# Four instead of six plain feature groups in a two-layer spectral and dense kernel, with regrouped quads and reordered row transfers

## The chip, the cores and the metric

The kernel runs on one core of one Trainium2 chip. The metric is the device time of one execution in microseconds, lower is better. The span of a profile runs from the first to the last instruction on the core; the execution's time is a little longer.

## What is computed

Two layers, each a spectral part and a dense part, on a residual stream x of 2048 tokens by 1024 features in bf16:

```python
x = x + _A_ref(_layernorm(x, axis=-1), A_w_r, A_w_i)
x = x + _B_ref(_layernorm(x, axis=-1), B_w1, B_b1, B_w2)
x = x + _A_ref(_layernorm(x, axis=-1), A_w_r, A_w_i)
x = x + _B_ref(_layernorm(x, axis=-1), B_w1, B_b1, B_w2)

def _A_ref(x, w_r, w_i):
    X = rfft2(x.astype(float32), axes=(-2, -1))
    return irfft2(X * (w_r + 1j * w_i), s=(S, D), axes=(-2, -1)).astype(bfloat16)

def _B_ref(x, w1, b1, w2):
    h = einsum("bsd,df->bsf", x, w1) + b1
    sp = log1p(exp(-abs(h))) + where(h > 0, h, 0)
    return einsum("bsf,fd->bsd", h * tanh(sp), w2)
```

The dense part has 3584 hidden features. Its activation is one table function (Mish) on ACT.

## The kernel before

The order of the work is written out by hand. A `Prog` object per engine collects instructions in program order; every tile has a `Res` that remembers who wrote and read it, and from these the waits follow. So each engine (and SP, which issues most DMAs, and POOL, which issues some and also computes) is one in-order queue, and an instruction's place in the program is its place in the queue.

**Spectral part** (`layer_A`). Stages of small matrix products. The first, `s1` (L635 on PE, evictions L641 on ACT and L643 on DVE), reads the tile XR, which holds all tokens in another order; the last, the inverse transform `i4` (L1020), reads the tile UT, 32 KB per partition from offset 64 K. `i4` for tokens 0 to 511 comes first; the rest (`rest`, fifteen or ten columns at a time) is woven into the beginning of the dense part, and its results go through the staging tile YS into the residual stream (`residual`, L1396).

**Dense part** (`layer_B`). Tokens are in four chunks of 512. Pass 0 covers chunks 0 and 1, pass 1 chunks 2 and 3. In each pass the first product makes 14 feature groups of 256 features. There are two ways to make a group:

- *plain*: `mm1` (L1148), 16 matmuls of 512 columns for each chunk, so 32 a group; a chunk can be halved into 256 columns. Three PSUM banks rotate, and ACT's Mish (L1152) empties them.
- *quad*: `quads` (L1186), a scheme of Strassen's kind with seven products of four matmuls, 28 a group. The products are named by their operands: A11*B11, A12*B21, A22*T4, S2*T2, S4*B22, S1*T1, S3*T3. A are quarters of the group's weights, S1 to S4 are sums of such quarters, B are parts of the two chunks, T1 to T4 are differences of such parts. A11*B11 and A12*B21 read chunk 0 alone. DVE makes T1 to T4 (`token_sums`, L1163). T3 is written over part of chunk 1. Each quad has one p1 copy on ACT (L574), five adds on DVE (L1191) and four Mishes on ACT (L1196).

The weight sums S1 to S4 of a group are made once, by POOL (L1081, four operations), in a slot of 7168 bytes that holds weights and sums, and stored to scratch; later passes load the slot from scratch. `fill_slot` does all of this. In layer 0, pass 0 makes the groups that it takes as quads, and pass 1 makes the others. POOL's first sums of pass 0 wait for a gate: DVE's last normalization of chunk 1. Slots WE0 to WE3 lie where UT lay, WS0 to WS2 where the plain groups' weights lie.

In pass 0 before the change, groups 0 to 5 are plain and 6 to 13 are quads. Chunk 1 is being normalized and transposed while chunk 0 is multiplied. Normalization of a tile of 128 tokens needs statistics (on DVE with bn_stats, L472, or on ACT with two summing passes, `stats_act`, L453), scales (8 small DVE operations, L502 to L515; after ACT statistics three more, L464 to L466), and `apply` (L524). Then the tile is transposed by PE (`transposed`, L1109, evicted by DVE, L1114) or by eight DMAs on SP (`turned` and `turn`).

Then `products` makes the second product (L1268) in seven stages of four tiles; a helper `extra` runs between its tiles.

**The boundary between the layers.** At the end of layer 0, each tile is normalized and stored as rows to scratch (`xn_store`, POOL), and loaded from there into XR (`xr_load`, SP). The last tile, 15, goes to XR directly in sixteen small DMAs (`xr_direct`, half k by block h). `xr_load(14)` waits for the store of tile 14. Meanwhile `spin` runs matmuls that nobody reads on PE.

```python
1601:                b = self.apply(j, out=True)
1602:                if j < 15:
1603:                    self.xn_store(j, b)
1604:                if j > 8:
1605:                    self.xr_load(j - 1)
1606:                if j == 15:
1607:                    self.xr_direct(j, b, 2, (pool, act, sp))
```

## Time and profile before

| what | us |
|---|---|
| median of 9 runs | 938.07 (936.67 to 940.18) |
| profiled execution | 936.9 |
| its span | 935.1 |
| mean granted TensorE clock | 0.989 |

| stage of layer 0 (us from the span's start) | from | to |
|---|---|---|
| plain groups of pass 0, chunk 0 and 1 | 123.7 | 173.5 |
| quads of pass 0 | 173.5 | 220.3 |
| second product of pass 0 | 220.3 | 307.6 |
| quads of pass 1 | 307.6 | 392.3 |
| second product of pass 1 | 397.1 | 478.5 |
| idle PE after the spin, layer boundary | 483.8 | 489.3 |

The costliest groups of instructions, as the page lists them (line, engine, operation, output from inputs, count; then busy time and mean duration in ns; then the engine's idle time ahead of them and what ended most of it):

```profile
L1268 PE MATMUL PS<-ARENA 128*128 128x512 bf16 x1536 | 338.0, 379 | 1.7
L1186 PE MATMUL PS<-ARENA 128*128 128x512 f16 (+1 forms) x1210 | 266.6, 379 | 2.1 <-POOL ARENA L1081 1.0
L1191 DVE TENSOR_TENSOR ARENA<-PS,ARENA 128x512 f32<-128x512 f32 x220 | 151.7, 691 | 96.2 <-PE PS L1186 92.1
L1196 ACT ACTIVATE ARENA<-ARENA,B 128x512 bf16<-128x512 f32 x132 | 95.0, 721 | 67.2 <-DVE ARENA L1191 61.1
L1148 PE MATMUL PS<-ARENA 128*128 128x256 bf16 (+1 forms) x570 | 86.7, 308 | 0.5
L1081 POOL TENSOR_TENSOR ARENA<-ARENA 128x512 bf16<-128x512 bf16 x56 | 71.3, 1274 | 73.8 <-DVE ARENA L524 59.0
```

Matmuls overlap, so their mean of 379 ns is a latency; the distance between two of them is shorter. Idle time of an engine that others don't wait for costs nothing.

### The profile page before, as it was taken

The page shows a single profiled execution, that of the slowest core. Times are in us where ns is not written, and L with a number is a line of the kernel's source. Part 1 is how long each engine was busy: PE and PEld are TensorE (multiplying, and loading weights), DVE is VectorE, ACT ScalarE, POOL GpSimd, SP SyncE. Part 2 cuts the span into 40 slices and gives each one's busy share as a digit, 9 for nine tenths or more (in the row PEclk, how much of TensorE's full clock was granted, in tenths as well). Part 3 has the DMA queues.
Part 4 walks back from the last instruction along what each step waited for, and adds up shares of the span by engine and source line. Part 5 has one row for each costly group of instructions (what it writes and reads, how often), then busy time and mean ns, then how long its engine had stood idle before and what let it go on. Part 6 is the DMA issues. An engine that isn't in the chain of part 4 may idle for free.

```text
span 935.1 us, 13406 instructions
## 1 busy us (share of the span) xinstructions
PE 871.5 (93%) x5398; PEld 471.7 (50%) x5473; DVE 618.9 (66%) x973; ACT 427.4 (46%) x623; POOL 158.4 (17%) x183
## 2 busy tenths in 40 slices
PE   0799789999999999999978987999999999999998
PEld 0676476444444444444437765754444444444443
DVE  7697468686889667568746865647746665554473
ACT  7798486456203475420008975745551015552000
POOL 3922003960004641010130200000000000000000
PEclk9999999999999999999989998999999999999999
DMA  9969854675796388364640798333155635832442
GB/s 289 265 222 295 206 139 126 215 273 144 259 277 230 139 309 292 116 242 142 252 149 32 223 228 198 158 118 119 54 187 170 213 113 191 279 120 77 169 127 112
DMA packets 146335, 174.68 MB, mean 187 GB/s; under 512 B 66248, under 2 KB 125736, under 8 KB 146152
## 3 DMA queue, kind: packets, MB, share of 16 engines
q1 hardware_dynamic: 133424, 127.48, 44.6%
q0 software_dynamic: 10672, 44.67, 13.3%
q10 hardware_dynamic: 2176, 1.66, 0.6%
q8 instruction: 43, 0.70, 0.3%
q14 instruction: 20, 0.16, 0.1%
HBM read 130.00 MB, written 40.89 MB: 183 GB/s over the span
## 4 chain that ended last, share of the span: by engine, by line
PE 81%; DMA 6%; DVE 5%; POOL 3%; ACT 2%; issue 1%; SPq 1%; POOLq 0%; DVEq 0%; ACTq 0%
PE PS L1268 34%; PE PS L1186 26%; PE PS L1148 9%; POOL ARENA L1081 2%; PE PS L799 2%; PE PS L725 2%; PE PS L1020 2%; PE PS L824 2%; DMA ARENA<-in_B_w_dram 1%; PE PS L1109 1%; DMA XS<-in_A_x_dram 1%; DMA ARENA<-c_bt 1%; POOL ARENA L251 1%; DMA ARENA<-u_scratch 1%; ACT ARENA L641 1%
## 5 line engine op out<-in xcount | busy, mean ns | idle before, releaser
L1268 PE MATMUL PS<-ARENA 128*128 128x512 bf16 x1536 | 338.0, 379 | 1.7
L1186 PE MATMUL PS<-ARENA 128*128 128x512 f16 (+1 forms) x1210 | 266.6, 379 | 2.1 <-POOL ARENA L1081 1.0
L1268 PEld LDWEIGHTS PS<-ARENA 128*128 128x128 bf16 x1568 | 153.3, 98 | 184.6 <-DVE ARENA L1311 0.3
L1191 DVE TENSOR_TENSOR ARENA<-PS,ARENA 128x512 f32<-128x512 f32 x220 | 151.7, 691 | 96.2 <-PE PS L1186 92.1
L1186 PEld LDWEIGHTS PS<-ARENA 128*128 128x128 bf16 x1232 | 120.2, 98 | 147.2 <-POOL ARENA L1081 2.6
L1196 ACT ACTIVATE ARENA<-ARENA,B 128x512 bf16<-128x512 f32 x132 | 95.0, 721 | 67.2 <-DVE ARENA L1191 61.1
L574 ACT ACTIVATE ARENA<-PS 128x512 f32<-128x512 f32 (+2 forms) x82 | 61.1, 745 | 119.2 <-PE PS L1186 96.4
L1148 PE MATMUL PS<-ARENA 128*128 128x256 bf16 (+1 forms) x570 | 86.7, 308 | 0.5
L1081 POOL TENSOR_TENSOR ARENA<-ARENA 128x512 bf16<-128x512 bf16 x56 | 71.3, 1274 | 73.8 <-DVE ARENA L524 59.0
L453 ACT ACTIVATE ARENA<-XS 128x1024 bf16<-128x1024 bf16 x52 | 54.8, 1053 | 37.0 <-DVE XS L1319 33.0
L1148 PEld LDWEIGHTS PS<-ARENA 128*128 128x128 bf16 x576 | 55.5, 98 | 26.7 <-DVE ARENA L1114 0.9
L1293 DVE TENSOR_TENSOR ARENA<-ARENA 128x3584 bf16<-128x3584 bf16 x32 | 63.9, 2016 | 0.0
L1319 DVE TENSOR_TENSOR XS<-PS,ARENA 128x512 bf16<-128x512 f32 x52 | 35.7, 689 | 38.5 <-PE PS L1268 38.2
L1152 ACT ACTIVATE ARENA<-PS,B 128x256 bf16<-128x256 f32 (+1 forms) x72 | 38.4, 542 | 35.6 <-PE PS L1148 35.0
L1311 DVE TENSOR_TENSOR ARENA<-PS,ARENA 128x512 f32<-128x512 f32 x48 | 32.9, 687 | 28.4 <-PE PS L1268 28.0
L1196 ACT ACTIVATE ARENA<-PS,B 128x512 bf16<-128x512 f32 x44 | 30.2, 686 | 18.0 <-PE PS L1186 18.0
L1307 DVE TENSOR_TENSOR ARENA<-ARENA,XS 128x512 f32<-128x512 f32 x52 | 36.7, 730 | 0.5
L1163 DVE TENSOR_TENSOR ARENA<-ARENA 128x2048 f16<-128x2048 bf16 x16 | 25.3, 1581 | 17.6 <-PE PS L1148 17.3
L799 PE MATMUL PS<-ARENA 128*128 128x256 bf16 x256 | 32.4, 273 | 4.2 <-DVE ARENA L788 3.2
L472 DVE BATCH_NORM_STATS2 BN<-XS 128x6 f32<-128x512 bf16 x52 | 32.7, 671 | 4.7 <-DMA XS<-in_A_x_dram 4.7
L444 ACT ACTIVATE RS<-MV,EPS 128x1 f32<-128x1 f32 (+2 forms) x11 | 3.3, 296 | 70.7 <-DVE MV L565 70.0
L777 ACT ACTIVATE ARENA<-PS 128x1024 bf16<-128x1024 f32 x32 | 33.3, 1071 | 4.5 <-PE PS L773 4.5
(97 smaller groups left out, 815.0 us busy)
## 6 DMA issues: line engine op xcount, KB each, us to landing
ARENA<-in_B_w_dram SPq DMA_DIRECT2D x30, 896.0 KB, 6.4
ARENA<-w1s_scratch SPq DMA_DIRECT2D x30, 896.0 KB, 4.8
ARENA<-w2s_scratch SPq DMA_DIRECT2D x24, 896.0 KB, 6.6
ARENA<-in_B_w_dram SPq DMA_DIRECT2D x26, 512.0 KB, 5.3
w1s_scratch<-ARENA POOLq DMA_DIRECT2D x14, 896.0 KB, 4.3
u_scratch<-ARENA SPq DMA_DIRECT2D x14, 512.0 KB, 3.5
ARENA<-u_scratch SPq DMA_DIRECT2D x14, 512.0 KB, 5.7
w2s_scratch<-ARENA POOLq DMA_DIRECT2D x8, 896.0 KB, 4.2
```

The costliest lines, as they stand in the source:

```text
L453: self.op(act, lambda e, i=i, f=f: e.activation(junk.ap, x, f, accum_out=sums[:, i:i + 1]), reads=[self.r_xs[j]], writes=[junk.res], parts ...
L574: fn = (lambda e: e.activation(dst, src, ACT.Copy)) if scale is None else \
L799: fns.append(lambda e, c=c, part=part: e.matmul(ps[:, c * 256:(c + 1) * 256], yk.ap[:, part, c * P:(c + 1) * P], t[:, (128, 0)[part]:(384, ...
L1081: self.op(self.pool, lambda e, dst=A(dst), x=A(x), y=A(y), op=op: e.tensor_tensor(dst, x, y, op), reads=[b.res] + list(after), writes=[b.rs])
L1148: fns.append(lambda e, db=db, bank=bank, fl=fl: e.matmul(PS[:, bank, 0:w], wb.ap[:, db, fl * P:(fl + 1) * P], x.ap[:, db, tok], start=(db ...
L1152: self.op(act, lambda e, bank=bank, ft=ft, at=at: e.activation(at[:, tok], PS[:, bank, 0:w], ACT.Mish, bias=self.B1[:, ft:ft + 1]), reads= ...
L1186: self.group([lambda e, db=db: e.matmul(PS[:, bank, :], A[:, db, :], mov[:, db, :], start=(start and db == 0), stop=(db == 3), skip_group_ ...
L1191: self.op(dve, lambda e: e.tensor_tensor(dst.ap, PS[:, bank, :], x.ap, ALU.add), reads=[self.r_bank[bank], x.res], writes=[dst.res])
L1196: self.op(act, lambda e: e.activation(at, src, ACT.Mish, bias=self.B1[:, ft:ft + 1]), reads=[res, self.r_b1], writes=[ra])
L1268: self.group([lambda e, i=i, k=k, b=PB[n][k].ap: e.matmul(PS[:, bank, :], ap[:, i, t * P:(t + 1) * P], b[:, i - 7 * k, :], start=(start an ...
L1293: self.op(dve, lambda e: e.tensor_tensor(ap[dst][:, f, :], ap[x][:, f, :], ap[y][:, f, :], op), reads=part(x, k) + part(y, k), writes=part ...
L1307: self.op(dve, lambda e: e.tensor_tensor(a[t], a[t], x, ALU.add), reads=[rx], writes=[r[t]])
```

## The change

Pass 0 of both layers: groups 0 to 3 are plain, 4 to 13 are quads.

- The places of plain groups 4 and 5 on chunk 0 are taken by the one-chunk products of quads 0 to 3: A11*B11 of all four (`block`) and A12*B21 of quads 1 to 3 (`corner`), in banks 3, 4, 5 and 0; the corner of quad 0 stays in its quad. Two more p1 buffers hold their copies.
- Slots WE0 to WE3 get their raw weights right after the last `rest` (`fill_raw`), and their sums behind the gate as before (`fill_sums`). For that UT's resource is split into four quarters by address.
- Products that read no sum no longer wait for the sums, in all passes.
- Tiles 6 and 7 have their residual ahead of 4 and 5, and their ACT statistics one group earlier. The transposes of tiles 6 and 7 stand in the third plain group of chunk 1 instead of the second.
- Tiles 8 to 11 have their statistics on ACT instead of DVE and their scales in two pairs; in layer 0 the residuals of tiles 10 and 11 move into the quads.
- In layer 1 tiles 13 and 14 are transposed by DMA instead of PE; before, in both layers, 13 to 15 are PE's.
- At the boundary `xr_direct(15)` is issued ahead of `xr_load(14)`, with another order of queues, and the spin has 38 matmuls instead of 24.

The core of the diff:

```diff
 def xr_direct(self, j, b, parts, queues):
+        b.unread = False
...
-            self.r_ut = self.sub_res(self.UT, "ut", 4, o["UT"], P * P * 2)
+            self.r_ut = [self.sub_res(self.UT, f"ut{q}", 1, o["UT"] + P * 64 * q, P * 64)[0] for q in range(4)]
...
-        self.w1_buf = [... for i in range(6)]
-        for fg in range(6):
+        self.w1_buf = [self.alloc(f"W1_{i}", self.ob["WS"] + i * 4096, [8, 256]) for i in range(4)]
+        for fg in range(4):
...
+    def fill_raw(self, b, fg):
+        r = self.r_w1d[fg]
+        if r.writes:
+            self.dma(self.sp, b.ap[:, 0:2048], self.w1s_d[fg][:, 0:2048], f"w1_{b.res.name}", reads=[r], writes=[b.res])
+        else:
+            self.load_w1(b.raw, fg, [b.res])
+    def fill_sums(self, b, fg, after):
+        r = self.r_w1d[fg]
+        if r.writes:
+            self.dma(self.sp, b.ap[:, 2048:3584], self.w1s_d[fg][:, 2048:3584], f"w1s_{b.res.name}", reads=[r], writes=[b.rs])
+        else:
+            self.w1_sums(b, fg, after)
...
+            p1_of = sums[0:2] + [self.alloc(f"P1_{off}", off, [512], F32) for off in spare]
+            ready = range(len(p1_of)) if spare else ()
...
-                            for db in range(4)], reads=[s.res, s.rs] + list(res), writes=[self.r_bank[bank]])
+                            for db in range(4)], reads=[s.res] + [s.rs] * (a[0] == "S") + list(res), writes=[self.r_bank[bank]])
...
+            def block(n, bank=None):
+                a, b, d, p1, u2, u3, ft = parts(n)
+                a = a if bank is None else bank
+                product(n, a, "A11", "B11", True)
+                self.copy(act, p1.ap, PS[:, a, :], [self.r_bank[a]], [p1.res])
+            def corner(n, bank=None):
+                a, b, d, p1, u2, u3, ft = parts(n)
+                a = a if bank is None else bank
+                product(n, a, "A12", "B21", False)
+                mish(0, ft, PS[:, a, :], self.r_bank[a])
...
+                        if n not in ready:
+                            block(n)
                         product(n, b, "S2", "T2", True)
...
                         product(n, d, "S1", "T1", True)
+                        if n not in ready:
+                            corner(n)
+                        elif n == 0:
+                            corner(0, 3)
                         product(n, b, "S3", "T3", False)
...
-        for j in range(4, 8):
+        early = self.open_slots("WE", self.ob["W2"], 0, 1, 2, 3)
+        for n in range(4):
+            self.fill_raw(early[n], 4 + n)
+        for j in (6, 7, 4, 5):
             residual(j)
...
             mm1(0, fg, 1)
-            if fg > 1:
-                self.stats_act(4 + fg)
-        mm1(0, 4)
+            if fg < 3:
+                self.stats_act(5 + fg)
         at_tiles(1)
-        mm1(0, 5, mid=turns(1, 0, 1))
+        block, corner, run = quads(list(range(4, 14)), order, B, [k * 1024 for k in (102, 140)])
+        for n, bank in ((0, 3), (1, 4), (2, 5), (3, 0)):
+            block(n, bank)
+        corner(1, 4)
+        for f in turns(1, 0, 1):
+            f()
+        corner(2, 5)
+        corner(3, 0)
...
-            self.fill_slot(early[n], 6 + n, [gate])
-        for fg in range(2):
-            mm1(1, fg, 0, mid=turns(1, 2, 3) if fg else ())
-        for fg in range(2):
+            self.fill_sums(early[n], 4 + n, [gate])
+        for fg in range(3):
+            mm1(1, fg, 0, mid=turns(1, 2, 3) if fg == 2 else ())
+        for fg in range(3):
             mm1(1, fg, 1)
...
         def after(n):
-            if n == 0:
-                self.fill_slot(order[7], 13)
+            if n in (0, 4, 5):
+                k = (7, 8, 9)[(0, 4, 5).index(n)]
+                self.fill_slot(order[k], 4 + k)
...
-            if n < 4:
-                self.stats_dve(8 + n)
-            if n == 4:
-                self.scales(8, 4)
-            if n > 3:
-                normal(4 + n)
+            if n in (0, 2, 4, 5):
+                self.stats_act(8 + (0, 2, 4, 5).index(n))
...
+            if n in (5, 7):
+                self.sums_to_mv(n + 3, 2)
+                self.scales(n + 3, 2)
+            if n > 5:
+                normal(2 + n)
                 turn(4)
-            for j in ((), (), (), (), (), (12, 13), (14,), (15,))[n]:
+            for j in {2: () if last else (10,), 4: () if last else (11,), 7: (12, 13), 8: (14,), 9: (15,)}.get(n, ()):
                 residual(j)
...
+        by_pe = 15 if last else 13
...
-                normal(12)
-                for j in (13, 14, 15):
+                for j in range(12, by_pe):
+                    normal(j)
+                for j in range(by_pe, 16):
                     xn[j] = self.apply(j)
...
+                else:
+                    self.xr_direct(j, b, 2, (act, pool, sp, act, pool, act, pool, sp) * 2)
                 if j > 8:
                     self.xr_load(j - 1)
-                if j == 15:
-                    self.xr_direct(j, b, 2, (pool, act, sp))
...
-            self.spin(24, 7)
+            self.spin(38, 7)
```

## The prediction

> **What bounds the kernel now.** I read the busy shares, then PE's waits, then the timeline of each engine around pass 0 of the dense stage in layer 0 (114 to 222 us; the same stage of layer 1 lies 455 us later), then the chain of waits at the layer boundary (478 to 500 us).
>
> The page's busy line, then who made PE wait:
>
> ```profile
> PE 871.5 (93%) x5398; PEld 471.7 (50%) x5473; DVE 618.9 (66%) x973; ACT 427.4 (46%) x623; POOL 158.4 (17%) x183
> ...
> PE PS L635 <- DMA ARENA<-ARENA: 5.4, 1, 5.4
> ...
> PE PS L1186 <- POOL ARENA L1081: 1.0, 3, 0.4
> ```
>
> The timelines of ACT, POOL and DVE (start, us, instruction):
>
> ```profile
> 142.59 1.05 ACT L453 ACTIVATE ARENA<-XS 128x1024 bf16<-128x1024 bf16 x1
> ...
> 144.82 0.82 ACT L1152 ACTIVATE ARENA<-PS,B 128x256 bf16<-128x256 f32 x2
> ...
> 154.06 6.57 POOL L1081 TENSOR_TENSOR ARENA<-ARENA 128x512 bf16<-128x512 bf16 x4 [58.99 <-DVE ARENA L524]
> ...
> 173.77 2.50 DVE L1163 TENSOR_TENSOR ARENA<-ARENA 128x2048 f16<-128x2048 bf16 x1 [5.82 <-PE PS L1148]
> ...
> 628.77 1.23 DVE L1163 TENSOR_TENSOR ARENA<-ARENA 128x2048 f16<-128x2048 bf16 x1 [11.46 <-PE PS L1148]
> ...
> 667.75 1.28 DVE L1396 TENSOR_TENSOR XS<-XS,ARENA 128x1024 bf16<-128x1024 bf16 x2
> 669.28 1.42 DVE L1191 TENSOR_TENSOR ARENA<-PS,ARENA 128x512 f32<-128x512 f32 x2 [0.24 <-PE PS L1186]
> ```
>
> The chain of waits at the boundary, and one row of PE's busy time by windows (behind the counts: clock, DMA share, GB/s):
>
> ```profile
> 481.97 0.60 SPq L251
> ...
> 483.20 5.85 DMA ARENA<-ARENA
> ...
> 486.50:488.00 1.50, 0.00 (x0) 0.00 (x0) 0.00 (x0) 0.00 (x0) 0.00 (x0) 0.50 0.82 164
> ```
>
> The reader is to see: PE is the bound (93%), so a matmul saved is time saved unless another engine makes PE wait. In the dense stages it waits for almost nothing, 1.0 us in all for POOL's sums. Each tile's ACT statistics hold ACT 2.23 us (142.59 to 144.82). POOL makes the four sums of a group in 4.87 us (a later row), and in 6.57 while DVE works on bf16 too; DVE's last token sum takes 2.50 us beside POOL and 1.23 alone. After a quad's third add, DVE has about 2 us before the next pair of adds. At the boundary PE is idle 5.45 us and restarts at half clock (0.50).
>
> **What the skill says.** The Trainium skill, *TensorE: Matmul & The Clock Gate*, Part 1, gives 215.7 ns for a warm matmul of 512 columns: here DVE's pairs of adds recur every 6.04 us in the quads (651.15 to 657.19), which is 28 matmuls at 0.216. It also says that the gate judges activity in free-running windows of 3413 ns; the clock here stays at half until about 493.0, one full window after work resumes. *SBUF — State Buffer*, "SBUF: two separate sides", says that VectorE and GpSimd share a port pair as an exclusive lock; 2.50 against 1.23 us agrees. *DMA: Bandwidth & Descriptors*, "Queues, rings and completion order", says that each engine consumes a queue's descriptors in ring order; in the trace SP's small row packets mostly come after the 32 KB packets of the load issued ahead of them.
>
> **The change, part by part.** I call four matmuls of 512 columns a product: 0.863 us.
>
> *Plain work saved, each layer.* Two groups of pass 0 go from plain (32 matmuls) to quads (28): 8 x 0.2158 = -1.73 us.
>
> *ACT statistics a group earlier.* Tile 6's now follow group 1's Mishes on ACT, tile 7's group 2's. ACT is free at 140.94; tile 6 occupies it to 143.17, and group 2's first Mish ends near 143.6. The fourth group's second half reuses that Mish's bank (mm1 rotates three) and would start at 142.87. Queued behind the statistics: both Mishes of group 2, hence PE. Wait +0.8 per layer (0.4 to 0.9). The p1 copies that follow (0.5 each) finish just as the corner product needs them. The transposes of tiles 4 and 5 then stand at 148.9, as before, after DVE's apply (148.15).
>
> *Early raw loads.* Slots 0 and 1 load while the inverse transform still runs; 2 and 3 wait for its last product (138.5). Two 0.5 MB loads, by a row of 5.3 us landing, are there near 144.5; blocks 2 and 3 need them at 145.4 and later. Cost 0, up to 1 without that cover. Splitting UT's resource is what lets 0 and 1 go; the split fill, the ring flag and the closures issue no other work.
>
> *T3 in layer 0.* T3 overwrites chunk 1's data, so it waits for the last plain product. Four products (3.45 us) cover T3 and the add behind it today; the block is gone, three remain (2.59). T3 2.42 to the next start, 0.29 delay, add 0.68: 3.4. Wait +0.4 to +0.85; I take +0.6, since POOL's gap for a store issue (0.56) falls there. Layer 1: 1.23 in place of 2.42, covered.
>
> *Short quads.* Quads 1 to 3 have five products (4.32 us). A22 of the quad before waits for an add that ends 0.92 after S3, and only S2 (0.86) lies between: 3 x 0.09 = +0.27 per layer (0 to 0.5). ACT and DVE otherwise fit: five adds are 3.45.
>
> *POOL in layer 0.* Its gate stays at 153.97, the sums still take 5.75 us a group with the store issue, but the quads start at 166.5 instead of 173.5 and the short ones need a slot each 4.4 us. POOL: slots done near 160.6, 167.5, 173.4, 179.2, 185.1; PE wants them at 166.5, 170.6, 175.0, 179.4, 184.7. Wait about +0.6 at quads 3 and 4, with the later ones just in time (0 to 6, see the rival). Block and corner products no longer wait for sums.
>
> *Scales by pairs.* After quad 7, DVE gets 11 small operations (0.198 each, 2.18), an apply (0.46) and two residuals (1.28) in one gap: 3.92 us from phase 4.05 of a 6.04 us period, so the next adds start 1.87 late. Block and S2 give them 0.75 to 0.8 of slack. +1.08 per layer (0.8 to 1.9; more if POOL still sums then, but its last sums end near 214.2, and the residuals start near 215.5). After quad 5 the lateness is 0.2 to 0.7, inside the slack. DVE loses four tiles' bn_stats and ACT gains 9 us, inside its idle 54%, with copies up to 1.2 us later, which the next adds absorb.
>
> *Pass 1 of layer 0.* Groups 4 and 5 now come from scratch instead of POOL, and A11 no longer waits for its sums: PE's three waits (0.35, 0.36, 0.26) go, -0.97. What is late next: sums for S2, 0.86 later, and they are there.
>
> *Tiles 13 and 14 by DMA in layer 1.* PE loses 16 transposes of 0.0557: -0.89. SP gains 16 DMA transposes at 1.28 us (16 took 20.49), two per 3.02 us of products, ahead of a weight load at most two: 2.6 us of the 12 us lead that a load has. Cost 0; if it failed, up to 2.6 a stage.
>
> *Boundary.* In SP's queue the row DMAs of tile 15 move ahead of tile 14's load, which waited for a store to land (481.95). SP now issues four at 481.8 to 484.2, ACT six, POOL six, as early as tile 15 is normalized (481.47). But tile 14's load (all rows of XR need it) now issues at 484.26, not 481.97. The load before took 3.6 us from issue, that one 4.7, so it lands at 487.9 to 489.0, against 489.05 for the last row today. PE starts near 488.65: -0.65 (-1.3 to +0.3). Spin: 38 instead of 24 (0.216 each) ends at 486.86 instead of 483.84. Idle shrinks from 5.45 to about 1.8 us. The window ending at 486.16 had 1.09 us of PE work and led to half clock; windows with 1.7 to 1.9 of work elsewhere did not (two with about that much, but of 32-column matmuls, did). I expect full clock. Then the first products come out at 0.43, not 0.86, per eviction, ACT starts 0.83 earlier and loses its 0.68 gap: -1.5 (0 to -1.55). After that ACT, not PE, bounds the stage.
>
> **Sum.** Layer 0, pass 0: -1.73 + 0.8 + 0.6 + 0.27 + 0.6 + 1.08 = +1.62. Its pass 1: -0.97. Boundary: -0.65 - 1.5 = -2.15. Layer 1: -1.73 + 0.8 + 0.27 + 1.08 - 0.89 = -0.47. Together -1.97 us. The profiled span 935.1 becomes 933.1, its execution 936.9 (1.8 outside the span) 934.9. The median of the runs is 938.07, so 936.1. That is -0.21%: on the edge of what a measurement tells, since about 0.2% (1.9 us) is the least it can tell from no change.
>
> **Rivals.**
> - *The boundary gives nothing* (937.9 to 938.3): tile 14's load lands as late as the rows did, and the window with 1.8 us of idle still drops the clock. For it: that load issues 2.3 us later. Against it: its 32 KB packets no longer wait behind the load before it. 938.07 - 1.97 + 2.15 = 938.25.
> - *POOL becomes the bound of pass 0 in layer 0* (slower). Place: S2 of quads 2 to 5. If DVE's token sums, residuals and T3, now packed into POOL's first five groups, keep each at 6.3 us plus 0.9 for its store, slot 4 is done at 154.06 + 5 x 7.2 - 0.9 = 189.2 instead of 185.1, against 184.7 wanted: 4.5 us of wait, not 0.6. Point of decision: above about 6.2 us a group, issue included, waits outgrow the gains. For it: the first group took 6.57. Against it: the third and fifth took 4.9. 936.1 + 3.9 = 940.
> - *My new waits are not there* (933): the ACT and scales waits are each read off in-order queues; if slack that I don't see hides half of the 5.5 us of added waits, 936.1 - 2.8 = 933.3.
>
> **How the numbers follow.** Forecast 0.50, of which 0.30 below 936.2 and 0.20 within 0.2%. Boundary gives nothing: 0.20 (0.02 faster, 0.14 same, 0.04 slower). POOL: 0.17 (0.02 same, 0.15 slower). Waits missing: 0.13, faster. Faster 0.45, same 0.36, slower 0.19. The forecast's own range, from the bounds, is 934.5 to 937.6; taking in the other cases until 2 in 10 is left out: 933.3 to 939.4.
>
> **What would show it.** Right: a wait of PE L1148 for ACT of about 0.8 per layer; one for DVE's adds of about 1.1 in the last quad; L1186 on POOL below 1.2 in layer 0's pass 0 and none in pass 1; clock 1.00 through the boundary; 16 PE transposes fewer. Wrong: POOL waits above 3 us, half clock after the spin, PE starting later than 10.8 us after the last product, or waits on raw weights or on DMA transposes.

## The result and the profile after

| | before | after |
|---|---|---|
| median of the runs, us | 938.75 (32 runs) | 942.36 (10 runs) |
| ratio, 95% interval | | 1.0047 (1.0034 to 1.0059) |
| profiled execution, its span, us | 936.9, 935.1 | 945.9, 944.1 |
| mean granted clock | 0.989 | 0.984 |
| layer 0: end of `rest` to second product of pass 0 | 81.59 | 88.23 |
| layer 1: the same | 81.59 | 82.02 |
| quads of pass 1, layer 0 | 84.37 | 82.88 |
| second product of pass 0, layer 1 | 87.67 | 86.78 |
| last product of layer 0 to first product of layer 1 | 10.79 | 11.84 |

The change makes the kernel slower by 0.47%; 936.1 had been forecast. The stages are read off PE's timeline. Three of them are as forecast or better; pass 0 of layer 0 lost 6.64 us, where +1.62 was forecast. (The rest of the difference between the two spans lies ahead of the dense parts, 1.9 us in layer 0 and 1.3 in layer 1. In layer 0 the first dense product of kernels with the change started anywhere from 122.6 to 125.9 us, over instructions that are the same in all of them, and in layer 1 two profiles of the kernel before differ by 1.1 there. So neither can be read as an effect of the change.)

The groups of the page that answer to those of before (line numbers are the changed kernel's: L1210 is L1186 of before, L1215 is L1191, L1170 L1148, L1103 L1081):

```profile
L1210 PE MATMUL PS<-ARENA 128*128 128x512 f16 (+1 forms) x1320 | 293.6, 381 | 7.0 <-DVE ARENA L1215 5.7
...
L1215 DVE TENSOR_TENSOR ARENA<-PS,ARENA 128x512 f32<-128x512 f32 x240 | 162.6, 690 | 105.3 <-PE PS L1210 95.6
...
L1103 POOL TENSOR_TENSOR ARENA<-ARENA 128x512 bf16<-128x512 bf16 x56 | 71.0, 1268 | 73.1 <-DVE ARENA L524 60.0
...
L1170 PE MATMUL PS<-ARENA 128*128 128x256 bf16 (+1 forms) x478 | 60.2, 282 | 1.5 <-ACT ARENA L1174 1.2
```

PE's idle time ahead of the quads went from 2.1 to 7.0 us, and its main releaser from POOL's sums to DVE's adds. The plain product got its wait for ACT. POOL's sums are no releaser at all any more. PE's waits by releaser (total, times, longest) say how few places these are, and the timeline of PE in pass 0 of layer 0 says where:

```profile
PE PS L1210 <- DVE ARENA L1215: 5.7, 4, 3.1
PE PS L636 <- DMA ARENA<-xn_scratch: 3.5, 1, 3.5
```

```profile
145.61 1.05 PE L1170 MATMUL PS<-ARENA 128*128 128x256 bf16 x8 [0.62 <-ACT ARENA L1174]
...
172.39 34.13 PE L1210 MATMUL PS<-ARENA 128*128 128x512 f16 x153 [1.06 <-DVE ARENA L1215]
209.64 13.95 PE L1210 MATMUL PS<-ARENA 128*128 128x512 f16 x55 [3.12 <-DVE ARENA L1215]
224.37 4.49 PE L1210 MATMUL PS<-ARENA 128*128 128x512 f16 x20 [0.78 <-DVE ARENA L1215]
```

The brackets hold the idle time ahead of a row. A matmul's own latency (0.379) reaches beyond its pitch (0.216), so a wait costs PE 0.16 more than is listed: the four here are 0.78, 1.22, 3.28 and 0.94. The first is ACT's statistics, the second T3, the fourth the scales after quad 7: all three forecast. The third, after quad 5, had been put at nothing. This is what DVE did just before it:

```profile
203.26 1.01 DVE L466 TENSOR_TENSOR MV<-MV,RS 128x2 f32<-128x2 f32 x1
204.30 0.17 DVE L502 TENSOR_SCALAR RS<-MV 128x2 f32<-128x2 f32 x1
204.51 0.17 DVE L504 TENSOR_SCALAR RS<-RS 128x2 int32<-128x2 int32 x1
204.71 1.61 DVE L513 TENSOR_TENSOR RS<-RS 128x2 f32<-128x2 f32 x1
206.36 0.16 DVE L514 TENSOR_TENSOR RS<-RS 128x2 f32<-128x2 f32 x1
206.55 1.00 DVE L515 SCALAR_TENSOR_TENSOR RS<-RS 128x2 f32<-128x2 f32 x1
...
207.78 1.00 DVE L514 TENSOR_TENSOR RS<-RS 128x2 f32<-128x2 f32 x1
...
208.90 2.61 DVE L1215 TENSOR_TENSOR ARENA<-PS,ARENA 128x512 f32<-128x512 f32 x4
```

These operations move two numbers a partition. Four of the eleven take 1.0 to 1.6 us, the others 0.16 to 0.18, and the same line is in both kinds. The eleven fill 202.85 to 208.97. In layer 1 they fill 664.14 to 666.27, each 0.16 or 0.17, and the eight of before were as short. Changed kernel in layer 1, then before in layer 0:

```profile
665.13 0.16 DVE L513 TENSOR_TENSOR RS<-RS 128x2 f32<-128x2 f32 x1
```

```profile
206.65 0.16 DVE L513 TENSOR_TENSOR RS<-RS 128x4 f32<-128x4 f32 x1
```

What differs beside them is POOL, here in the changed kernel, then its last sums in this pass before:

```profile
199.37 4.88 POOL L1103 TENSOR_TENSOR ARENA<-ARENA 128x512 bf16<-128x512 bf16 x4
...
205.13 4.87 POOL L1103 TENSOR_TENSOR ARENA<-ARENA 128x512 bf16<-128x512 bf16 x4
...
210.87 4.99 POOL L1103 TENSOR_TENSOR ARENA<-ARENA 128x512 bf16<-128x512 bf16 x4
```

```profile
197.84 4.87 POOL L1081 TENSOR_TENSOR ARENA<-ARENA 128x512 bf16<-128x512 bf16 x4
```

POOL now sums ten groups in this pass instead of eight and is at it until 215.9; before it was done at 202.7, and the scales began at 206.25. Four of POOL's operations in 4.87 us are 1.22 each, about the length of a long one of DVE's. Last, the clock: PE's idle 3.3 us is followed by a stretch at half speed (of a table of windows, the column behind the POOL count is the granted clock):

```profile
210.50:212.00 1.50, 1.50 (x5) 0.61 (x4) 1.01 (x2) 1.03 (x2) 1.48 (x2) 0.50 0.46 188
212.00:213.50 1.50, 1.50 (x5) 0.46 (x3) 1.02 (x2) 0.56 (x2) 1.34 (x3) 0.50 1.02 411
214.00:216.00 2.00, 2.00 (x11) 0.91 (x10) 0.14 (x1) 0.69 (x1) 1.78 (x2) 1.00 0.09 24
```

The granted clock is 0.50 from 210.5 to 213.9, which makes 3.4 us of products take twice as long as they should: 1.7 us.

### The profile page after: what moved, and what is told of

Same layout as the page of the kernel before. It is cut to its first block, busy times and chain, and to the rows that moved or that the text cites. A ratio compares the mean times of both kernels' runs of the same rounds, so it can differ in the third digit from the quotient of the medians.

```text
span 944.1 us, 13518 instructions
## 1 busy us (share of the span) xinstructions
PE 875.2 (93%) x5412; PEld 475.2 (50%) x5487; DVE 625.9 (66%) x997; ACT 443.8 (47%) x661; POOL 158.0 (17%) x183
## 4 chain that ended last, share of the span: by engine, by line
PE 79%; DVE 9%; DMA 5%; ACT 4%; issue 1%; POOL 1%; SPq 1%; ACTq 0%; DVEq 0%; POOLq 0%
PE PS L1309 35%; PE PS L1210 29%; PE PS L1170 4%; PE PS L800 2%; PE PS L726 2%; PE PS L1021 2%; PE PS L825 2%; DMA XS<-in_A_x_dram 1%; PE PS L1131 1%; DMA ARENA<-u_scratch 1%; DMA ARENA<-c_bt 1%; DVE ARENA L1185 1%; POOL ARENA L251 1%; ACT ARENA L642 1%; DMA u_scratch<-ARENA 1%
## 5 line engine op out<-in xcount | busy, mean ns | idle before, releaser
L1210 PE MATMUL PS<-ARENA 128*128 128x512 f16 (+1 forms) x1320 | 293.6, 381 | 7.0 <-DVE ARENA L1215 5.7
L1215 DVE TENSOR_TENSOR ARENA<-PS,ARENA 128x512 f32<-128x512 f32 x240 | 162.6, 690 | 105.3 <-PE PS L1210 95.6
L1210 PEld LDWEIGHTS PS<-ARENA 128*128 128x128 bf16 x1344 | 130.8, 98 | 167.2 <-DVE ARENA L1215 11.8
L1220 ACT ACTIVATE ARENA<-ARENA,B 128x512 bf16<-128x512 f32 x144 | 102.9, 720 | 77.1 <-DVE ARENA L1215 72.2
L453 ACT ACTIVATE ARENA<-XS 128x1024 bf16<-128x1024 bf16 x68 | 71.6, 1052 | 37.6 <-DVE XS L1360 33.0
L1103 POOL TENSOR_TENSOR ARENA<-ARENA 128x512 bf16<-128x512 bf16 x56 | 71.0, 1268 | 73.1 <-DVE ARENA L524 60.0
L1170 PE MATMUL PS<-ARENA 128*128 128x256 bf16 (+1 forms) x478 | 60.2, 282 | 1.5 <-ACT ARENA L1174 1.2
L1352 DVE TENSOR_TENSOR ARENA<-PS,ARENA 128x512 f32<-128x512 f32 x48 | 33.0, 688 | 30.6 <-PE PS L1309 30.2
L1170 PEld LDWEIGHTS PS<-ARENA 128*128 128x128 bf16 x480 | 46.3, 99 | 11.4 <-ACT ARENA L1174 1.8
L1220 ACT ACTIVATE ARENA<-PS,B 128x512 bf16<-128x512 f32 x48 | 32.9, 685 | 19.5 <-PE PS L1210 19.5
L1174 ACT ACTIVATE ARENA<-PS,B 128x256 bf16<-128x256 f32 (+1 forms) x60 | 28.5, 485 | 21.0 <-PE PS L1170 20.9
L782 DVE TENSOR_TENSOR ARENA<-ARENA 128x1024 bf16<-128x1024 bf16 x32 | 22.0, 687 | 20.0 <-ACT ARENA L778 20.0
L726 PE MATMUL PS<-FD,ARENA 128*128 128x256 bf16 (+1 forms) x256 | 31.8, 271 | 2.5 <-ACT ARENA L642 1.3
```

Source lines behind the costliest of these rows:

```text
L453: self.op(act, lambda e, i=i, f=f: e.activation(junk.ap, x, f, accum_out=sums[:, i:i + 1]), reads=[self.r_xs[j]], writes=[junk.res], parts ...
L726: fns.append(lambda e: e.matmul(dst, at(r), FD[:, t:t + n], start=start, stop=stop))
L1103: self.op(self.pool, lambda e, dst=A(dst), x=A(x), y=A(y), op=op: e.tensor_tensor(dst, x, y, op), reads=[b.res] + list(after), writes=[b.rs])
L1170: fns.append(lambda e, db=db, bank=bank, fl=fl: e.matmul(PS[:, bank, 0:w], wb.ap[:, db, fl * P:(fl + 1) * P], x.ap[:, db, tok], start=(db ...
L1210: self.group([lambda e, db=db: e.matmul(PS[:, bank, :], A[:, db, :], mov[:, db, :], start=(start and db == 0), stop=(db == 3), skip_group_ ...
L1215: self.op(dve, lambda e: e.tensor_tensor(dst.ap, PS[:, bank, :], x.ap, ALU.add), reads=[self.r_bank[bank], x.res], writes=[dst.res])
```

## The experiments

All are edits of the changed kernel, unless said otherwise, and their ratios are to the kernel before. "Pass 0" means the stretch from the end of `rest` to the second product, which in the changed kernel is 88.23 in layer 0 and 82.02 in layer 1. It repeats to 0.01 us in layer 1 of six kernels with the same order there, so small terms can be read from it where the ratio can't. In layer 0 the five kernels that leave it as it is took 88.23 to 89.49, since the wait after quad 5 was 3.1 to 3.7 us in them and the half clock behind it lasted 3.4 or 6.8. So a difference of less than about 1.3 us between single profiles tells nothing there, unless this wait and this half clock are alike in both.

### Is it POOL that stretches the small operations?

**One input in SBUF.** In layer 0, tiles 8 and 9 are scaled one at a time, after quads 5 and 6, by nine `tensor_scalar` operations that have only one tensor operand, the others being one number a partition. For one tile they are also narrower: all but the first move one number a partition instead of two.

```diff
+    def scales_one(self, j):
+        mv, sums, rr = self.MV[:, j, :], self.BN[:, j, 0:2], [self.r_rs[j]]
...
+        on(a, mean, mean, None, op0=ALU.mult)
+        on(var, var, a, None, op0=ALU.subtract)
...
+            on(a, r, r, h, op0=ALU.mult, op1=ALU.mult)
+            on(r, a, 1.5, r, op0=ALU.subtract, op1=ALU.mult)
...
-            if n in (5, 7):
+            if n in (5, 6) and not last:
+                self.scales_one(n + 3)
+            elif n in (5, 7):
```

> In layer 0 alone, tiles 8 and 9 get their scales one tile at a time (after quads 5 and 6) and by nine operations with one SBUF tensor input each (the other operands are scalars per partition), in place of eleven with mostly two inputs after quad 5; POOL goes on with its sums. Lock theory (two-input DVE operations wait for POOL's running operation): no DVE operation of the scales is longer than 0.25 us, PE's wait of 3.1 us for DVE's adds near 209 us goes, with it the dip of the clock there; 4 to 5 us less than the changed kernel in layer 0's pass 0, so 0.0 to -0.1% against before. Length theory (the scales are simply too long for the gap, in whatever form): 18 operations of 0.2 are 3.6 us in place of 2.2, spread over two gaps; the wait shrinks at most by half, time stays at +0.2 to +0.5%. ACT theory (the adds are late since the p1 copy is late behind ACT's statistics): the wait stays near 3 us, +0.47%.

Ratio 1.0003 (0.9994 to 1.0012). Pass 0 of layer 0 is 84.07, 4.16 us less, and there is no stretch at half clock in it. POOL summed from 198.61 to 203.48 and from 204.36 to 209.25. DVE's first nine operations, most of them beside it, by DVE's timeline:

```profile
202.03 0.24 DVE L524 TENSOR_SCALAR MV<-BN 128x2 f32<-128x2 f32 x1
202.31 0.21 DVE L524 TENSOR_SCALAR RS<-MV 128x1 f32<-128x1 f32 x1
202.55 0.21 DVE L524 TENSOR_SCALAR MV<-MV,RS 128x1 f32<-128x1 f32 x1
202.80 0.15 DVE L524 TENSOR_SCALAR RS<-MV 128x1 f32<-128x1 f32 x1
202.99 1.27 DVE L524 TENSOR_SCALAR RS<-RS 128x1 int32<-128x1 int32 x5
204.18 1.41 DVE L1232 TENSOR_TENSOR ARENA<-PS,ARENA 128x512 f32<-128x512 f32 x2
```

None stands still, nor does one of the second nine (from 208.08). This one edit takes back nearly all that the change had lost. Whether the one input or the one column is what helps, this run alone doesn't tell.

**POOL idle.** The scales as they are, but POOL doesn't make the sums of groups 11 and 12 in pass 0 of layer 0, so these groups are multiplied with what stood in their slots.

```diff
-                              ("S4", "A12", "S2", ALU.subtract)):
+                              ("S4", "A12", "S2", ALU.subtract)) * (not self.no_sums):
...
+                self.no_sums = k in (7, 8) and not last
                 self.fill_slot(order[k], 4 + k)
+                self.no_sums = False
```

> The changed kernel, but in layer 0's pass 0 POOL leaves out the sums of groups 11 and 12 (these two groups are multiplied with stale sums), so that POOL computes nothing between about 199 and 210 us, where DVE makes the first pair of scales; the DVE operations are those of the changed kernel. Lock theory: the eleven operations take 0.2 us each, 2.2 in all, as in layer 1; PE's wait of 3.1 us goes to below 0.3, 4 to 5 us less than the changed kernel. Length and ACT theories: DVE's scales and PE's wait stay as they are, since DVE and ACT have the same work.

Ratio 0.9996 (0.9986 to 1.0006). Pass 0 of layer 0 is 83.25, 4.98 us less. The eleven operations take 0.16 or 0.17 each (200.51 to 202.64), with two inputs as before; two of those that had stood still in the changed kernel (L513 and L515 there):

```profile
201.50 0.16 DVE L514 TENSOR_TENSOR RS<-RS 128x2 f32<-128x2 f32 x1
...
201.89 0.16 DVE L516 SCALAR_TENSOR_TENSOR RS<-RS 128x2 f32<-128x2 f32 x1
```

So neither their number nor their place after quad 5 made the loss.

**POOL busy in layer 1.** This is the opposite: six sums that nobody reads are put on POOL beside the scales of layer 1, where the cost was not.

```diff
+            if n == 5 and last:
+                busy = self.alloc("BUSY", 102 * 1024, [4, P])
+                tail = Res("tail")
+                tail.set_w(dve, dve.count)
+                x, y = self.wblock(order[6], "A11"), self.wblock(order[6], "A21")
+                for _ in range(6):
+                    self.op(pool, lambda e: e.tensor_tensor(busy.ap, x, y, ALU.add),
+                            reads=[order[6].res, tail], writes=[busy.res])
```

> The changed kernel with one cost added where it was not: in layer 1, where POOL does nothing in the quads, six sums of 128x512 bf16 are put on POOL, starting with the first pair of scales after quad 5, written to a place that nobody reads. Theory (each small operation of DVE with two inputs in SBUF stands still while POOL's operation runs): the eleven small operations, 2.1 us from first start to last end in layer 1 of the changed kernel (664.14 to 666.27), take about 6 us, as in layer 0, a wait of PE for DVE's adds of about 3 us appears there, pass 0 of layer 1 is 2.5 to 3.5 us longer, and the ratio to before rises from 1.0047 to about 1.008. Rival (something else in layer 0 slows the scales there): they stay at 2.1 us and the ratio at 1.0047.

Ratio 1.0094 (1.0076 to 1.0111). Pass 0 of layer 1 is 85.65, 3.63 us more. DVE, POOL and PE there, by their timelines:

```profile
660.02 1.14 DVE L465 TENSOR_TENSOR RS<-MV 128x2 f32<-128x2 f32 x1
661.20 0.16 DVE L466 TENSOR_TENSOR MV<-MV,RS 128x2 f32<-128x2 f32 x1
661.39 1.01 DVE L502 TENSOR_SCALAR RS<-MV 128x2 f32<-128x2 f32 x1
662.44 0.17 DVE L504 TENSOR_SCALAR RS<-RS 128x2 int32<-128x2 int32 x1
662.64 0.99 DVE L513 TENSOR_TENSOR RS<-RS 128x2 f32<-128x2 f32 x1
```

```profile
660.00 7.32 POOL L1548 TENSOR_TENSOR ARENA<-ARENA 128x512 bf16<-128x512 bf16 x6 [115.78 <-DVE MV L464]
```

```profile
666.95 12.26 PE L1210 MATMUL PS<-ARENA 128*128 128x512 f16 x55 [3.46 <-DVE ARENA L1215]
```

Every second operation stands until POOL's current one is over: two small operations go through for each 1.22 us of POOL's, so eleven last 6.5 us, and the wait of layer 0 is made again in layer 1. POOL pays nothing: its six take 1.22 each. One that stood still, L502, has a single tensor input, so "two inputs" is not the whole rule for what can be blocked. All fourteen profiles together say what the one-tile form has that helps. Of the small operations with one input that ran beside POOL's sums, the 41 that move one number a partition took 0.28 at most, as without POOL; of the 20 that move two or four, nine took 0.31 to 1.01, where without POOL none took more than 0.18. So what got through goes with the single column, and not with the single input alone.

### The other waits of pass 0 in layer 0

**T3.** Quad 0 keeps its own A11*B11, and the one-chunk product A12*B21 of quad 2 goes ahead of the transposes.

```diff
-            ready = range(len(p1_of)) if spare else ()
+            ready = (1, 2, 3) if spare else ()
...
-        for n, bank in ((0, 3), (1, 4), (2, 5), (3, 0)):
+        for n, bank in ((1, 4), (2, 5), (3, 0)):
             block(n, bank)
         corner(1, 4)
+        corner(2, 5)
         for f in turns(1, 0, 1):
             f()
-        corner(2, 5)
```

> Quad 0 keeps its block product (A11*B11) behind the last plain product; quads 1 to 3 give theirs early, and the corner of quad 2 goes ahead of the transposes of tiles 4 and 5 in its stead. Same products. Theory: the block again covers T3 in layer 0, PE's wait of 1.06 us for DVE's add near 172 us goes to 0 to 0.2, about 1.1 us less than the changed kernel in layer 0 and nothing in layer 1; +0.35% against before. Rival (the wait is for something else than T3, or the wait moves to the corner products): no change of the sum.

The forecast was missed: the ratio is 1.0054 (1.004 to 1.0068). PE's waits by releaser:

```profile
PE PS L1210 <- DVE ARENA L1215: 5.2, 3, 3.7
...
PE PS L1170 <- ACT ARENA L1174: 1.2, 2, 0.6
PE PS L1210 <- ACT ARENA L1174: 1.1, 2, 0.5
...
PE PS L1210 <- POOL ARENA L1103: 0.2, 1, 0.2
```

The wait for T3 is gone (three waits for adds instead of four), but PE now meets ACT's statistics a second time in each layer (0.5) and comes to POOL's sums early once. Pass 0 is 0.87 longer in layer 1, where T3 had cost nothing. In layer 0 it is 0.57 longer, which is within what this stretch varies by, and so is the longest wait at the scales (3.7 for 3.1). A wait removed ahead of another limit moved PE to that limit.

**Residuals behind the scales.** The residuals of tiles 12 and 13 are moved so that none stands in the gap with the second pair of scales.

```diff
-            for j in {2: () if last else (10,), 4: () if last else (11,), 7: (12, 13), 8: (14,), 9: (15,)}.get(n, ()):
+            for j in {2: () if last else (10,), 4: () if last else (11,), 6: (12,), 8: (13, 14), 9: (15,)}.get(n, ()):
```

> The residuals of tiles 12 and 13 leave the gap after quad 7, where they stand behind the second pair of scales and an apply: tile 12 goes to the gap after quad 6, 13 to that after quad 8. Same operations. Theory (that gap holds 3.9 us of DVE work and the adds behind it come late): PE's wait of 0.78 us for DVE's adds in the last quad goes in both layers, about 1.8 us less than the changed kernel (0.94 a layer), +0.25 to +0.3%. Rival (the wait comes from the scales alone): 0.78 stays.

Ratio 1.0026 (1.0014 to 1.0038). Both waits of 0.78 are gone; pass 0 is 0.91 shorter in layer 0, with the wait after quad 5 (3.16) and its half clock (3.4) as in the changed kernel, and 0.96 in layer 1. This cost was as forecast, and a change of order avoids it. In this profile 0.48 of it came back in layer 1's second product, as a wait for a weight load; the mended kernel below has such a wait too, and the one with another boundary has none.

**ACT's statistics a group later.**

```diff
-            if fg < 3:
-                self.stats_act(5 + fg)
+            if fg == 2:
+                self.stats_act(6)
...
         corner(1, 4)
+        self.stats_act(7)
```

> Against the changed kernel one thing is moved in both layers: ACT's statistics of tile 6 stand behind the third plain group and those of tile 7 behind the one-chunk products of the first quads, instead of one group earlier each. Theory (the statistics that stand ahead of group 2's Mishes hold up PE): the wait of the plain product for ACT (two of 0.6 us in the changed kernel) goes, the ratio to the kernel before falls from 1.0047 to about 1.003, if what follows tile 7's later scales still has slack. Rival (ACT's wait is only the first of two limits there): the time comes back as a wait of transposes or of chunk 1's plain groups for DVE's normalization, and the ratio stays at 1.0045.

Ratio 1.0038 (1.0022 to 1.0053), which can't be told from the changed kernel's. The wait for ACT is gone in both layers. In layer 1 pass 0 is 0.79 shorter, the full price. In layer 0 PE came earlier and then waited 0.73 for POOL's sums, which the changed kernel doesn't, so most of the gain was lost there. That pass 0 is even 1.40 longer in layer 0 can't be put down to the edit: the wait at the scales (3.64) and the half clock behind it (6.8) are as long in kernels that leave this stretch as it is.

### The boundary

**Rows last**, as before, with the longer spin.

```diff
-                else:
-                    self.xr_direct(j, b, 2, (act, pool, sp, act, pool, act, pool, sp) * 2)
                 if j > 8:
                     self.xr_load(j - 1)
+                if j == 15:
+                    self.xr_direct(j, b, 2, (pool, act, sp))
```

> The changed kernel with the boundary's order of before: tile 14's load is issued ahead of tile 15's sixteen row transfers, with their old three queues; the spin keeps its 38 matmuls. Theory (the four row transfers that SP issues ahead of the load, 0.6 to 0.74 us each, delay it, and it is what PE waits for): the first product after the spin starts about 10.8 us after the last product of layer 0, as before, not 11.84, and the ratio falls to about 1.0035. If the longer spin alone decides the clock, no window at half clock is left after it (another 1.5 us less); if the idle of 3 us that stays is what decides, it stays. Rival (the load isn't what is last): start unchanged at 11.8 and ratio 1.0045.

**Rows off SP.**

```diff
-                    self.xr_direct(j, b, 2, (act, pool, sp, act, pool, act, pool, sp) * 2)
+                    self.xr_direct(j, b, 2, (act, pool))
```

> The changed kernel with tile 15's sixteen row transfers on ACT's and POOL's queues alone, so that tile 14's load is the next thing on SP. Theory: that load issues about 2.5 us earlier (near 489.6 instead of 492.1 on the changed kernel's time line), the first product starts 8.5 to 9.5 us after the last one instead of 11.84, PE's idle falls below 1.5 us and the clock stays full; 2.5 to 4 us less, ratio about 1.001. Rival (the row transfers become last, as eight on a queue take longer than five or six): the start falls by less than 1 us, ratio 1.004.

**The kernel before, profiled again.**

> The kernel before, profiled a second time, nothing changed. It tells how far its own stages vary between executions. In the kernels with the change the first product of the dense part started between 122.6 and 125.9 us and the wait at the boundary was 11.0 to 12.1 us; before had 123.7 and 10.8 in its one profile. If the start varies with the execution and not with the change, it lies in the same two or three us here; if the boundary of before is really shorter, it is 10.6 to 11.0 here again. The half clock at the start of the dense stages had 6.8 us in before's one profile and 10.2 in most of the others: 10.2 here too means that it is no part of the change.

| kernel | last to first product, us | half clock over the first stage, us |
|---|---|---|
| before, twice | 10.79, 12.19 | 3.7, 5.7 |
| changed | 11.84 (11.50 to 12.22 in seven others with this order of transfers) | 3.2 |
| rows last | 11.04 | 3.4 |
| rows off SP | 10.98 | 3.4 |
| mended, and mended with another boundary (both below) | 11.31, 11.31 | 3.4, none |

Ratios: rows last 1.0052 (1.0035 to 1.0069), rows off SP 1.0039 (1.0025 to 1.0054); neither can be told from the changed kernel's. The execution of before that was profiled again took 939.3 us (span 937.5). Its boundary is longer than the changed kernel's, so the 1.05 us that the first two profiles show between them can't be put down to the change. The other orders, at 10.98 to 11.31, lie below all eight profiles of the changed one, but before itself, with the order of rows last, had 12.19, so a gain by order isn't shown. The chain of waits says why the order matters so little. Changed kernel, then rows off SP:

```profile
488.62 0.60 SPq L251
...
492.10 5.02 DMA ARENA<-xn_scratch
```

```profile
490.15 1.01 ACTq L251
...
491.19 5.26 DMA ARENA<-ARENA
```

In the changed kernel SP issues four rows between 489.27 and 492.05, and the load behind them is last. With the rows off SP that load was there by 495.6, and a row was last: the fourth on ACT's queue, the last there of the half that the first products read, 5.26 after its issue. (ACT's other four rows, of the second half, were the last transfers of all; ACT needed 7.2 us to issue its eight.) In before's two profiles it was a row as well, 5.85 and 6.23 after. Whichever transfer was last, it was issued 4.7 to 6.5 us after the last product and landed 5 to 6.2 us later. What sets these 5 to 6 us was not tried.

**A longer spin.**

```diff
-            self.spin(38, 7)
+            self.spin(50, 7)
```

> The changed kernel with 50 matmuls in the spin at the layer boundary instead of 38. It ends about 10.8 us after the last product, some 1 us ahead of the data. Theory of the prediction (the idle ahead of the first stage brings the half clock there): no window at half clock follows within 10 us, and from the stage's first matmul to its second part (24 matmuls of 256 columns) it takes about 9.6 us where it took 11.08; ratio about 1.003. Rival (ACT's evictions bound that stage at either clock): no half clock, but the stage keeps its 11.1 us and the ratio its 1.0047.

Ratio 1.0038 (1.0025 to 1.0051). PE, by its timeline:

```profile
484.23 10.95 PE L653 MATMUL PS<-BD 128*128 128x512 bf16 x49
496.44 6.83 PE L636 MATMUL PS<-M,ARENA 128*128 128x128 bf16 x104 [1.26 <-issue]
...
506.35 2.57 PE L726 MATMUL PS<-FD,ARENA 128*128 128x256 bf16 x24 [1.30 <-ACT ARENA L642]
```

The ratio can't be told from the changed kernel's, and the first product came 12.22 us after the last. With 1.26 us of idle no half clock follows, and the stage from 496.44 to 506.35 takes 9.91 us in place of 11.08: 1.2 us, of 1.5 expected. The clock part of the forecast was sound; its condition, an idle of 1.8 us after 38 spins, was not met (3.48 listed).

### All mends together

In both layers: one-input scales for tiles 8 to 11, quad 0 with its own block, statistics of tiles 6 and 7 later, the residuals of 12 to 15 after the last quad, rows off SP. The residuals of tiles 7 and 11, two buffers and a PSUM bank are moved to make room for this.

```diff
-            ready = range(len(p1_of)) if spare else ()
+            ready = (1, 2, 3) if spare else ()
...
-            if n in (0, 2, 4, 5):
-                self.stats_act(8 + (0, 2, 4, 5).index(n))
+            if n in (0, 2, 4, 6):
+                self.stats_act(8 + n // 2)
...
-            if n in (5, 7):
-                self.sums_to_mv(n + 3, 2)
-                self.scales(n + 3, 2)
+            if n in (4, 5, 7, 8):
+                self.scales_one(8 + (4, 5, 7, 8).index(n))
...
+            for j in {2: () if last else (10,), 3: () if last else (11,), 9: (12, 13, 14, 15)}.get(n, ()):
...
-                    self.xr_direct(j, b, 2, (act, pool, sp, act, pool, act, pool, sp) * 2)
+                    self.xr_direct(j, b, 2, (act, pool))
```

> All mends in one kernel, in both layers: tiles 8 to 11 scaled one at a time by operations with one input in SBUF after quads 4, 5, 7, 8, ACT statistics of tiles 6 and 7 later, the first quad keeps its block so that T3 is covered, residuals of 10 and 11 earlier and of 12 to 15 after the last quad, the row transfers of tile 15 on ACT and POOL. If the waits that the changed kernel got are what it lost by, their sum goes: against the changed kernel about 3.4 (scales) + 0.6 (T3) + 1.6 (ACT) + 1.6 (residuals) + 3 (boundary), some 10 us, so that the ratio to the kernel before is about 0.993. If they stand in for one another (one wait gone lets the next one grow), less than half of it comes: ratio 0.998 to 1.0.

933.25 us, ratio 0.9952 (0.9933 to 0.9971): faster than before and after. Pass 0 is 81.56 in layer 0, 6.67 less than in the changed kernel, and 80.43 in layer 1. PE's quads in pass 0 of layer 0 then have one wait left, by its timeline:

```profile
186.36 35.71 PE L1227 MATMUL PS<-ARENA 128*128 128x512 f16 x161 [0.73 <-POOL ARENA L1120]
```

The mends in the passes came through; that of the boundary didn't (11.31).

**The same with another boundary:** tile 14's load first, rows six on ACT, eight on POOL, two on SP, and a spin of 44.

```diff
-                    self.xr_direct(j, b, 2, (act, pool))
...
+                if j == 15:
+                    self.xr_direct(j, b, 2, (act, pool) * 6 + (sp, pool) * 2)
...
-            self.spin(38, 7)
+            self.spin(44, 7)
```

> The mended kernel, with another boundary: tile 14's load is issued ahead of tile 15's rows, these are six on ACT, eight on POOL and two on SP, and the spin has 44 matmuls. If what is last at the boundary is a queue that issues too many rows (eight on ACT took 6.2 to 7.2 us), the first product starts about 10.3 us after the last, against 11.31 in the mended kernel, and the ratio to before is about 0.994. If the transfers themselves are what is last, whichever queue they come from, it stays at 10.8 to 11.3 and the ratio at 0.995.

934.16 us, ratio 0.9954 (0.9938 to 0.997), no different from the mended kernel's. The start stays at 11.31; the half clock is gone, and the stage is 9.90 us long.

## Why the prediction was wrong

It named the right mechanisms and priced most of them well, but left the largest cost at nothing and counted on a gain at the boundary that isn't there.

| term, us | forecast | measured |
|---|---|---|
| plain work, layer 0 | -1.73 | -1.73 by count |
| ACT's statistics, layer 0 | +0.8 | +0.78; 0.79 by experiment (layer 1) |
| T3, layer 0 | +0.6 | +1.22 |
| short quads, layer 0 | +0.27 | +0.45, as what remains (0.44 in layer 1) |
| POOL's sums late | +0.6 | 0 |
| scales after quad 5, layer 0 | 0 | +3.28 |
| half clock after that wait | 0 | +1.7 |
| scales after quad 7, layer 0 | +1.08 | +0.94; 0.91 by experiment |
| pass 1 of layer 0 | -0.97 | -1.49 |
| boundary | -2.15 | about 0 |
| layer 1, pass 0 | +0.42 | +0.43 |
| DMA transposes, layer 1 | -0.89 | -0.89 |

- **The step that failed** is "After quad 5 the lateness is 0.2 to 0.7, inside the slack." It priced eleven small operations at 0.198 each from rows that ran with POOL idle. The prediction itself had POOL summing until 214.2 (it was 215.9), and knew the lock from the token sums (2.50 against 1.23). It asked what POOL does to the scales after quad 7 only, where POOL is done, and not after quad 5, ten microseconds earlier. Shown from three sides: other operations beside POOL (-4.16 us), no POOL beside the same operations (-4.98), and POOL put beside them in layer 1 (+3.63).
- *SBUF — State Buffer*, "SBUF: two separate sides", of the Trainium skill says that the loser of the lock blocks for the winner's whole instruction. The runs agree: in the two cases shown above, a blocked operation of 0.16 took 0.99 to 1.61 us, close to one of POOL's 1.22. What failed was pricing the lock as a stretch of large operations only.
- **The boundary.** "so it lands at 487.9 to 489.0", said of tile 14's load, is 9.4 to 10.5 us after the last product; it landed 11.54 after (497.12). It was issued 6.52 after the last product and not 5.76, as the four rows took 2.79 of SP's queue in place of 2.4 and began later, behind a load that waited for tile 13's store (5.49 to landing); and it took 5.02, the longer end. But the term was also read against one profile of before, whose 10.79 was a short one: the second had 12.19. At a place that varies by 1.4 between executions, a bound of -1.3 to +0.3 was too narrow. The -1.5 for the clock was right in kind (1.2 measured), but hung on the earlier start.
- **T3** was undersized: 1.22 for 0.6. **POOL's sums** weren't late, as T3's wait and ACT's come first; with these out of the way 0.73 of it came up in the mended kernel. **Pass 1** gained more than the three waits: 96 products at 0.863 are 82.88, no wait left.
- **Rivals.** That POOL becomes the bound was right about the engine and wrong about the way: not by late sums (no wait), but through DVE. "The boundary gives nothing" came true as well. The forecast of layer 1, where POOL is idle, was right to 0.01 us in sum, in part by luck: the short quads cost 0.17 more than forecast and the scales 0.14 less.
- The sum: pass 0 of layer 0 is 6.64 - 1.62 = 5.02 above its forecast, pass 1 0.52 below, the boundary 2.15 above, 6.65 in all. From -1.97 that gives +4.7; 0.47% of 938 is 4.4. Pass 0 of layer 0 is from one profile, and it varies by 1.3, so the two agree as far as can be told.

## What to carry to other kernels

Before small VectorE operations are moved, look up what GpSimd does at their new time: here each blocked one cost about a whole one of POOL's, so eleven of 0.16 us took 6, and the wait of over 3 us that this made on TensorE mostly drew a stretch of half clock on top. Work that is moved to an earlier place in a queue has to be judged against every later limit on the path: two of the mends, made alone, brought PE sooner to the next limit in layer 0, and all of them together gained. And a term that is read at a place that varies between executions needs a second profile of before.

## What the runs showed of the hardware that wasn't expected

- Operations of two elements a partition stood 0.99 to 1.61 us beside POOL's sums, five of eleven in the clearest case, in turn with free ones, while POOL's own stayed at 1.22. `tensor_scalar` operations of one column went through at 0.15 to 0.28, all 41 of them. Those of two columns did not always: the first of the nine took 0.24 in one kernel and 0.99 in another (195.81 in the mended one).
- Larger ones are hit too: a tile's `apply` took 1.44 in place of 0.54 beside POOL (at 210.14 with one-input scales), a residual 1.51 (at 189.75 in the mended kernel) in place of 0.68. DVE's adds from PSUM kept their 0.68 to 0.69.
- After the wait of 3.1 to 3.7 us on PE at the scales of layer 0, one or two windows of 3.4 us at half clock followed in all eight profiles of kernels that kept these scales beside POOL. The wait of 3.46 us made in layer 1 brought none, nor did 1.26 us at the boundary. Where a wait falls seems to decide, not its length alone. The edges of the half clock lie on a grid of 3.41 us: in the changed kernel it begins at 210.5, 497.2 and 579.1, which is 84 and then 24 steps on. By an estimate from PE's rows, the step of layer 0 ahead of 210.5 held 0.84 us of products. The wait in layer 1 fell on two steps, and these held 1.42 and 1.78. What share of a step is the limit was not tried.
